# Attention scores from three 64-row products on the two halves of the matmul array, instead of two 128-row products over the whole of it

## The chip, the cores and the metric

The kernel runs on one core of a Trainium2 chip. The metric is device microseconds of one execution, the median of a few runs. TensorE (PE) does the matmuls and loads their stationary operands (PEld), VectorE (DVE), ScalarE (ACT) and GpSimd (POOL) do elementwise work, and SP issues the transfers.

## The reference

Attention with pooled queries, then two feed-forward blocks on the same 1152 tokens. Everything is float32 (some weights come as float64).

```python
def _attn_ref(q, k, v):                     # [2, 8, 1152, 64] each
    q_pool = q.reshape(B, H, S // 2, 2, D).mean(axis=3)
    scores = scale * np.matmul(q_pool, k.transpose(0, 1, 3, 2))
    scores = scores - np.max(scores, axis=-1, keepdims=True)
    attn = np.exp(scores)
    attn = attn / (np.sum(attn, axis=-1, keepdims=True) + 1e-09)
    return np.matmul(attn, v)
...
x = attn_out as [1152, 512]
x = elu(x @ w_in) @ w_out                   # 512 -> 2048 -> 512
xn = x / sqrt(mean(x * x) + 1e-6) * rms_g
out = (silu(xn @ w_gate) * (xn @ w_val)) @ w_out2   # 512 -> 1536 -> 512
```

There are 16 heads with 576 pooled queries, 1152 keys and 64 features each.

## The kernel before

**Products in parts.** A float32 operand x is split into xh, which is x rounded to the matmul's reduced type float32r, and xl = x - xh. A product x*y is then xh*yh + xh*yl + xl*yh, and where it costs nothing also xl*yl.

**Pairs and steps.** Attention works on 8 pairs of heads. A pair has 9 query tiles of 128 rows (`TILES`): four of each head, and the tile M with 64 rows of both. That is 72 steps. Step n does this, in the order in which PE gets it:

1. `emit_S`: the scores of tile n (S, L280) in one buffer `s` of 3 PSUM banks. DVE then scales them into `p` and takes the row minimum (L284). The buffer is single, so the next S waits for this L284.
2. `do_T`: 9 transposes (T, L298) of tile n - 2's exponentials, into three banks `t`; per bank ACT writes the upper part `pth` (L306) and DVE the lower part `ptl` (L68).
3. `do_AV(8)`: up to 8 matmuls (A, L324) of P^T times V for a group of tiles. A group (`GROUPS`, four per pair) takes 18 of them, in one of two banks `o`.
4. `emit_exp` (L289, ACT), then the splitting of operands of the next pair (`plan`, `do_prep`, on POOL but for the first steps), and in the last 33 steps one operation of the weight stream `ws` (lines 113 to 142) per step.

The engines' programs are in the order in which the code emits them. Between two pairs, `emit_scale` adds five transposes (L359, L360).

**Scores before.** A head's features are 64, the array has 128 rows. Queries lie twice on the partitions, keys as the upper part on partitions 0 to 63 and the lower part on 64 to 127 (`prep_k`):

```python
        hi(d, t)
        lo(d[64:128], t[64:128], d[64:128])
```

One 128-row matmul of qh with them gives qh*kh + qh*kl, and one of ql gives the other two products. A tile needs two such over 1152 keys, in three banks of 384: 6 matmuls (12 for M). Each matmul loads its stationary operand anew. Keys come in two halves of 576 columns for all 128 partitions, each half split by two operations.

**PSUM.** 8 banks: 3 for `s`, 2 for `o`, 3 for `t`; while the first two steps run, `ps1` (a second `s`) lies where `t` will be.

**After attention** the last tiles' work is mixed with the first blocks of the first feed-forward layer (`early`), and the feed-forward blocks follow (from L168 on, with 8 banks in turn).

Of the kernel before, what the change touches and what calls it, by code (L numbers as in the profile page):

```python
# [8 lines left out]
F32 = mybir.dt.float32  # L9
F32R = mybir.dt.float32r  # L10
# [27 lines left out]
def tile_kernel(ctx: ExitStack, tc: tile.TileContext, qd, kd, vd, w1d, w2d, wgd, wvd, wod, rgd, outd):  # L38
# [31 lines left out]
    NE, WB = 3, 8      # pieces split during attention; buffers for pieces' parts  # L70
# [1 line left out]
    class Stream:  # L72
        """Pieces are worked on operation by operation, so that they fill the engines' gaps."""

        def __init__(self, srcs):
            self.srcs = srcs
            self.loaded = self.done = self.at = 0
            self.alloc = False      # the next operation allocates the parts of piece self.at
            self.raw, self.parts = {}, {}
            self.pools = [(wp, NE)]     # the parts of the pieces go round their buffers  # L80
            self.ops = self.work()
# [14 lines left out]
        def work(self):  # L96
            tail = None
            for i in range(len(self.srcs)):
# [4 lines left out]
                if wide:  # L103
                    # float64 as pairs of words -> float32, rounded to nearest: the upper word's bits in float32's
                    # places, and the lower word times the exponent's power of two; under 2^-126: 0 (the upper
                    # words, read as float32, are in the order of the magnitudes).
# [42 lines left out]
        def step(self, i, k):  # L149
            """Up to k operations, with piece i the first in use."""  # L150
# [12 lines left out]
    def product(out, w, a, first, last, ks=range(4)):  # L163
        """out += sum over 4 blocks of 128 rows of w^T a, w and a in parts; a(k): the parts of block k."""
# [16 lines left out]
    def elu(ps, gh, gl, lo):  # L181
        """g = max(h, exp(min(h, 0)) - 1) in parts."""
# [10 lines left out]
    w_out = [w2d[i] for i in range(16)]      # index quad * 4 + dm  # L193

    # =================== attention ===================
# [7 lines left out]
    pp = actx.enter_context(tc.tile_pool(name="psO", bufs=1, space=PSUM))  # L203
# [3 lines left out]
    # a head's queries in parts, with 64 columns of zeros before and after; those of the tile M come first (j = 1)  # L207
    # or last (j = 0)
# [11 lines left out]
    KD, VD, QD = {}, {}, {}     # (pair, j)  # L220

    def load(kind, p, j, half=0):
# [3 lines left out]
        elif kind == "k":  # L226
# [4 lines left out]
            SP.dma_start(out=t, in_=kd[2 * p + j][:, half * QS:(half + 1) * QS])  # L231
# [5 lines left out]
    def prep_q(p, j, t, eng, cols=((0, QS),)):  # L237
        """Sums of two queries in parts."""
# [10 lines left out]
    def prep_k(p, j, half, t, eng):  # L249
        hi, lo = eng  # L250
        if half == 0:
            KD[p, j] = ap.tile([128, S], F32R, tag="kd", name="kd", bufs=3)
        d = KD[p, j][:, half * QS:(half + 1) * QS]
        hi(d, t)
        lo(d[64:128], t[64:128], d[64:128])
# [9 lines left out]
    st = {}         # pair -> statistics tile: [0] -scale*max, [1] sum, [2] sum + eps, [3] 1 / sum  # L265
    P = {}
    xf = {}

    def emit_S(p, i):
        if i == 0:  # L270
            st[p] = ap.tile([128, 4, NPT, 1], F32, tag="st", name="st", bufs=2)
        s = (tp if (p, i) == (0, 1) else sp).tile([128, 3, 512], F32, tag="s", name="s", bufs=1)
        if i == M:
            parts = [(QD[p, j][:, u, c:c + 128], KD[p, j]) for j, c in ((1, 0), (0, 576)) for u in (0, 1)]
        else:
            j, c, _, _, _ = TILES[i]
            parts = [(QD[p, j][:, u, c:c + 128], KD[p, j]) for u in (0, 1)]
        for n, (a, b) in enumerate(parts):
            for m in range(3):
                PE.matmul(s[:, m, 0:384], lhsT=a, rhs=b[:, 384 * m:384 * m + 384],  # L280
                          start=n == 0, stop=n == len(parts) - 1)
        pt = P[p, i] = ap.tile([128, 3, 384], F32, tag="p", name="p", bufs=3)
        # -scale * scores, and the least of them (scale = 1/8, and 1/2 of the mean of two queries)
        V.tensor_scalar(out=pt, in0=s[:, :, 0:384], scalar1=-0.0625, scalar2=None,  # L284
# [24 lines left out]
    class AV:  # L309
        """P^T * V for a group: the product with the upper part of V on partitions 0-63, with the lower on 64-127."""  # L310
# [5 lines left out]
        def emit(self, k):  # L316
            g = self.g
            if self.n == 0:
                self.o = pp.tile([128, 512], F32, tag="o", name="o", bufs=2)
# [418 lines left out]
```

## Time and profile before

| | us |
|---|---|
| median of 3 runs (724.67 to 725.17) | 725.07 |
| span of the profiled execution, first to last instruction | 722.7 |
| around the span (difference of the two) | 2.4 |
| first L284 to last L284, 72 steps | 9.37 to 245.93 |

The runs of the profile page are timed from outside; its own time is not listed apart, and the span with 2.4 us around it stands for it. PE is busy 689.2 us of the span, DVE 614.9, ACT 415.6 and POOL 390.7; the busy time of PE counts overlapping instructions once and holds the modelled tail of each matmul. The granted TensorE clock is a share of 2.4 GHz.

### The profile page before, as it was taken

How to read it: one execution, taken by the hardware profiler on the slowest of the kernel's cores; microseconds unless marked ns; L12 is line 12 of the kernel's file. 1: busy time of each engine (PE TensorE's matmuls, PEld its weight loads, DVE VectorE, ACT ScalarE, POOL GpSimd, SP SyncE). 2: the span in 40 equal slices, each digit the busy share in tenths (PEclk: the TensorE clock that was granted, in tenths of full speed). 3: DMA queues.
4: the chain of work that ended last, by engine and by line, in shares of the span. 5: the costliest groups of instructions: out<-in, count | busy, mean ns of one | idle time of the engine just before them, and what ended most of it. 6: DMA issues, size and time to landing. Idle time of an engine off the chain costs nothing.

```text
span 722.7 us, 11547 instructions
## 1 busy us (share of the span) xinstructions
PE 689.2 (95%) x4243; PEld 673.3 (93%) x4243; DVE 614.9 (85%) x965; ACT 415.6 (58%) x855; POOL 390.7 (54%) x326
## 2 busy tenths in 40 slices
PE   7999999999999999969999968979999999999997
PEld 6999999989899999859999968979999999999997
DVE  7988989898999869999999999955999999999700
ACT  5888988889798865663356663424444443432300
POOL 4988889788896226754335453523445544443300
PEclk9999999999999999989999998989999999999999
DMA  5333322533331001223322212200222222222300
GB/s 196 116 96 135 98 84 83 172 131 107 105 98 48 1 30 60 87 70 105 117 92 85 87 59 88 88 30 1 87 88 89 88 88 88 88 88 88 124 34 33
DMA packets 21607, 62.34 MB, mean 86 GB/s; under 512 B 2736, under 2 KB 4784, under 8 KB 21552
## 3 DMA queue, kind: packets, MB, share of 16 engines
q1 hardware_dynamic: 21552, 61.62, 25.9%
q8 instruction: 33, 0.54, 0.3%
q14 instruction: 22, 0.18, 0.1%
HBM read 59.25 MB, written 2.36 MB: 85 GB/s over the span
## 4 chain that ended last, share of the span: by engine, by line
PE 74%; DVE 19%; ACT 3%; issue 3%; DMA 1%; SPq 0%; POOL 0%; DVEq 0%; ACTq 0%; POOLq 0%
PE b L169 15%; PE b L168 15%; PE b L170 15%; PE s L280 10%; PE o L324 9%; PE t L298 8%; DVE wt L121 3%; DVE wt L118 3%; DVE p L284 2%; DVE ptl L68 2%; DVE e L188 2%; DVE wx L124 2%; DVE wx L126 1%; DVE wt L130 1%; DVE wt L113 1%
## 5 line engine op out<-in xcount | busy, mean ns | idle before, releaser
L62 POOL TENSOR_TENSOR wl<-wt,wh 128x512 fp32r<-128x512 f32 x68 | 106.1, 1561 | 111.6 <-ACT wh L142 60.2
L168 PE MATMUL b<-xh,wh 128*128 128x384 f32 x468 | 157.7, 337 | 2.1 <-DVE e L188 1.5
L170 PE MATMUL b<-xh,wl 128*128 128x384 f32 x468 | 157.3, 336 | 0.0
L169 PE MATMUL b<-xl,wh 128*128 128x384 f32 x468 | 157.1, 336 | 0.0
L284 DVE TENSOR_SCALAR_CACHE_REDUCE p<-s 128x1152 f32<-128x1152 f32 x72 | 97.2, 1352 | 17.5 <-PE s L280 17.4
L68 DVE TENSOR_TENSOR ptl<-t,pth 128x384 fp32r<-128x384 f32 x216 | 106.5, 547 | 2.7 <-ACT pth L306 2.0
L280 PE MATMUL s<-kd,qt 128*128 128x384 f32 x480 | 98.6, 343 | 5.4 <-DVE p L284 4.8
L306 ACT CAST pth<-t 128x384 fp32r<-128x384 f32 x216 | 89.2, 488 | 24.1 <-PE t L298 23.5
L121 DVE SCALAR_TENSOR_TENSOR wt<-we,wt 128x512 f32<-128x512 f32 x68 | 95.5, 1404 | 4.5 <-ACT sqm L562 0.5
L289 ACT ACTIVATE p<-p,st 128x1152 f32<-128x1152 f32 x72 | 91.4, 1269 | 5.8 <-DVE p L284 5.5
L168 PEld LDWEIGHTS b<-xh,wh 128*128 128x128 f32 x468 | 88.0, 188 | 3.5 <-DVE e L188 2.5
L280 PEld LDWEIGHTS s<-kd,qt 128*128 128x128 f32 x480 | 81.5, 188 | 9.3 <-DVE p L284 6.5
L170 PEld LDWEIGHTS b<-xh,wl 128*128 128x128 f32 x468 | 88.0, 188 | 0.3 <-POOL wl L62 0.3
L169 PEld LDWEIGHTS b<-xl,wh 128*128 128x128 f32 x468 | 88.0, 188 | 0.0
L298 PE MATMUL t<-ident,p 128*128 128x128 f32 x648 | 85.3, 275 | 0.1
L324 PE MATMUL o<-pth,vd 128*128 128x256 f32 (+1 forms) x288 | 84.4, 315 | 0.0
L298 PEld LDWEIGHTS t<-ident,p 128*128 128x128 f32 x648 | 74.0, 141 | 6.3 <-DVE ptl L68 3.9
L324 PE MATMUL o<-ptl,vd 128*128 128x256 f32 (+1 forms) x288 | 78.5, 295 | 0.0
L168 PE MATMUL b<-gh,wh 128*128 128x384 f32 x180 | 64.3, 357 | 14.1 <-ACT gh L189 10.8
L142 ACT CAST wh<-wt 128x512 fp32r<-128x512 f32 x68 | 42.1, 619 | 59.5 <-DVE wt L130 58.4
L111 ACT ACTIVATE we<-wr 128x512 f32<-128x512 f32 x68 | 45.8, 674 | 47.2 <-DMA wr<-in_w_dram 16.1
L62 POOL TENSOR_TENSOR gl<-e,gh 128x384 fp32r<-128x384 f32 x37 | 46.8, 1265 | 41.4 <-ACT gh L189 39.7
(114 smaller groups left out, 1414.5 us busy)
## 6 DMA issues: line engine op xcount, KB each, us to landing
wr<-in_w_dram SPq DMA_DIRECT2D x32, 512.0 KB, 3.2
rawk<-in_k_dram SPq DMA_DIRECT2D x32, 288.0 KB, 2.9
rawq<-in_q_dram SPq DMA_DIRECT2D x15, 576.0 KB, 3.9
wr<-in_wg_dram SPq DMA_DIRECT2D x12, 512.0 KB, 3.2
wr<-in_wv_dram SPq DMA_DIRECT2D x12, 512.0 KB, 3.2
wr<-in_wo_dram SPq DMA_DIRECT2D x12, 512.0 KB, 3.3
rawv<-in_v_dram SPq DMA_DIRECT2D x16, 288.0 KB, 2.8
out_dram<-o SPq DMA_DIRECT2D x12, 192.0 KB, 1.9
```

The lines of the kernel that those rows point to most:

```text
L62: G.tensor_tensor(out=o, in0=i, in1=f(h), op=ALU.subtract)
L68: V.tensor_tensor(out=o, in0=i, in1=f(h), op=ALU.subtract)
L121: V.scalar_tensor_tensor(out=f(t), in0=e, scalar=TINY64 * TINY64, in1=f(t), op0=ALU.is_ge, op1=ALU.mult)
L168: PE.matmul(out, lhsT=wh[:, k, :], rhs=ah, start=first and k == 0, stop=False)
L169: PE.matmul(out, lhsT=wh[:, k, :], rhs=al, start=False, stop=False)
L170: PE.matmul(out, lhsT=wl[:, k, :], rhs=ah, start=False, stop=last and k == 3)
L280: PE.matmul(s[:, m, 0:384], lhsT=a, rhs=b[:, 384 * m:384 * m + 384], start=n == 0, stop=n == len(parts) - 1)
L284: V.tensor_scalar(out=pt, in0=s[:, :, 0:384], scalar1=-0.0625, scalar2=None, op0=ALU.mult, op1=ALU.min, accum_out=st[p][:, 0, TILES[i][4], :])
L289: T.activation(out=pt, in_=pt, func=AF.Exp, scale=-1.0, bias=st[p][:, 0, TILES[i][4], :], accum_out=st[p][:, 1, TILES[i][4], :])
L298: PE.transpose(ps[:, k, :], src[:, 128 * b:128 * b + 128], ident)
L306: T.copy(oh, re(ps))
L324: PE.matmul(self.o[:, 0:self.N], lhsT=v[:, b, :], rhs=(pth, ptl)[u][:, g["buf"], b, g["c0"]:320], start=self.n == 0, stop=self.n == 17)
```

## The change

Only attention's front half changes.

- **Scores.** `kd` is now [128, 2, 576]: on partitions 0 to 63 lie the first 576 keys, on 64 to 127 the other 576, each as upper (index 0) and lower part (index 1). A score is three products over 64 rows: qh*kh, qh*kl and ql*kh; ql*kl is gone. The products of the first 576 keys use partitions 0 to 63 of queries and keys, those of the others partitions 64 to 127, and they alternate in the program; they write different banks. 288 columns go into a bank, four banks to a tile: 12 matmuls of 288 columns with 64 rows, instead of 6 of 384 columns with 128 rows.
- **Keys.** One load of two 64-partition pieces and one split (two operations) per head, instead of two loads and two splits.
- **PSUM.** `s` has four banks, `o` one; `do_AV(9)` makes each group two equal portions. The feed-forward blocks turn over 4 + 4 banks, formerly 5 + 3.
- **Start.** The 24 transposes ahead of the first scores write a tile of `tp`.

```diff
-            SP.dma_start(out=t, in_=kd[2 * p + j][:, half * QS:(half + 1) * QS])
+            for h in range(2):
+                SP.dma_start(out=t[64 * h:64 * h + 64], in_=kd[2 * p + j][64 * h:64 * h + 64, QS * h:QS * h + QS])
...
-    def prep_k(p, j, half, t, eng):
+    def prep_k(p, j, t, eng):
         hi, lo = eng
-        if half == 0:
-            KD[p, j] = ap.tile([128, S], F32R, tag="kd", name="kd", bufs=3)
-        d = KD[p, j][:, half * QS:(half + 1) * QS]
-        hi(d, t)
-        lo(d[64:128], t[64:128], d[64:128])
+        d = KD[p, j] = ap.tile([128, 2, QS], F32R, tag="kd", name="kd", bufs=3)
+        hi(d[:, 0, :], t)
+        lo(d[:, 1, :], t, d[:, 0, :])
...
-        s = (tp if (p, i) == (0, 1) else sp).tile([128, 3, 512], F32, tag="s", name="s", bufs=1)
+        s = (tp if (p, i) == (0, 1) else sp).tile([128, 4, 512], F32, tag="s", name="s", bufs=1)
...
-        for n, (a, b) in enumerate(parts):
-            for m in range(3):
-                PE.matmul(s[:, m, 0:384], lhsT=a, rhs=b[:, 384 * m:384 * m + 384],
-                          start=n == 0, stop=n == len(parts) - 1)
-        pt = P[p, i] = ap.tile([128, 3, 384], F32, tag="p", name="p", bufs=3)
+        parts = [(QD[p, j][:, u, c:c + 128], KD[p, j][:, v, :]) for j, c in parts for u, v in ((0, 0), (0, 1), (1, 0))]
+        for m in range(2):
+            for n, (a, b) in enumerate(parts):
+                for h in range(2):
+                    r = slice(64 * h, 64 * h + 64)
+                    PE.matmul(s[:, 2 * h + m, 0:288], lhsT=a[r], rhs=b[r, 288 * m:288 * m + 288],
+                              start=n == 0, stop=n == len(parts) - 1)
+        pt = P[p, i] = ap.tile([128, 4, 288], F32, tag="p", name="p", bufs=3)
...
-                self.o = pp.tile([128, 512], F32, tag="o", name="o", bufs=2)
+                self.o = pp.tile([128, 512], F32, tag="o", name="o", bufs=1)
...
-        do_AV(8, lambda p: later.append((step + 2, lambda: emit_x(p, emit_scale(p)))))
+        do_AV(9, lambda p: later.append((step + 2, lambda: emit_x(p, emit_scale(p)))))
...
-    psb = [ctx.enter_context(tc.tile_pool(name="psB", bufs=5, space=PSUM))]
+    psb = [ctx.enter_context(tc.tile_pool(name="psB", bufs=4, space=PSUM))]
```

On PE, around the tile M of the first pair, the program before reads as follows (`s` are scores, `t` transposes, `o` products with V; the shape is that of the output):

```order
L324 MATMUL o<-ptl,vd 128x320
L280 MATMUL s<-kd,qt_93 128x384 x6
L280 MATMUL s<-kd,qt_91 128x384 x6
L324 MATMUL o<-pth,vd 128x320
L324 MATMUL o<-ptl,vd 128x320
L298 MATMUL t<-ident,p 128x128 x9
L324 MATMUL o<-pth,vd 128x256
```

The same place of the changed program:

```order
L326 MATMUL o<-ptl,vd 128x320
L282 MATMUL s<-kd,qt_90 128x288 x6
L282 MATMUL s<-kd,qt_88 128x288 x6
L282 MATMUL s<-kd,qt_90 128x288 x6
L282 MATMUL s<-kd,qt_88 128x288 x6
L300 MATMUL t<-ident,p 128x128 x9
L326 MATMUL o<-pth,vd 128x256
```

The 12 score matmuls of M have become 24, and the two left-over matmuls of a group that stood ahead of the transposes have gone into the portions of 9.

At the change from one pair to the next the program before has, on PE, four matmuls ahead of the transposes and then 8 in the next step; the first rows of the changed program at that place are these:

```order
L326 MATMUL o<-ptl,vd 128x256
L300 MATMUL t<-ident,p 128x128 x9
L282 MATMUL s<-kd,qt_88 128x288 x12
L300 MATMUL t<-ident,p 128x128 x9
L282 MATMUL s<-kd,qt_88 128x288 x12
```

So one step of each pair now holds scores and transposes alone, and the other eight hold 9 products with V each.

On POOL, the keys of a head take these four rows before, and the two rows below them now:

```order
L59 TENSOR_SCALAR kd<-rawk 128x576
L62 TENSOR_TENSOR kd<-rawk,kd 64x576
L59 TENSOR_SCALAR kd<-rawk 128x576
L62 TENSOR_TENSOR kd<-rawk,kd 64x576
```

```order
L59 TENSOR_SCALAR kd<-rawk 128x576
L62 TENSOR_TENSOR kd<-rawk,kd 128x576
```

The second operation now covers 128 partitions, and there is one of each instead of two.

## Rows read from the trace of the kernel before

**Rows 1.** The profile page: busy time of the engines, then the granted clock in 40 slices of the span, and the shares of the chain that ended last.

```profile
span 722.7 us, 11547 instructions
PE 689.2 (95%) x4243; PEld 673.3 (93%) x4243; DVE 614.9 (85%) x965; ACT 415.6 (58%) x855; POOL 390.7 (54%) x326
PEclk9999999999999999989999998989999999999999
PE 74%; DVE 19%; ACT 3%; issue 3%; DMA 1%; SPq 0%; POOL 0%; DVEq 0%; ACTq 0%; POOLq 0%
```

**Rows 2.** Busy time of each engine in two pairs of heads (one without weight operations on DVE, one with), and in the stretch of all steps with weight operations. Columns: stretch, its length, busy us of PE, PEld, DVE, ACT, POOL with instruction counts, granted clock, DMA share, GB/s.

```profile
72.42:102.30 29.88, 29.88 (x220) 29.09 (x219) 25.81 (x50) 25.55 (x55) 25.30 (x25) 1.00 0.31 100
191.86:222.96 31.10, 30.26 (x218) 28.90 (x217) 29.49 (x55) 26.64 (x57) 27.77 (x26) 1.00 0.35 112
138.40:245.93 107.53, 104.79 (x749) 99.50 (x748) 102.76 (x188) 92.55 (x199) 85.82 (x76) 1.00 0.27 90
```

**Rows 3.** DVE in order of time, the score evacuations that begin a stretch: start, duration, in brackets the idle time before it and who ended it. (The first, at 19.58, is that of step 4; those at 72.42 and 102.30 are one pair apart.)

```profile
19.58 1.36 DVE L284 TENSOR_SCALAR_CACHE_REDUCE p<-s 128x1152 f32<-128x1152 f32 x1 [0.80 <-PE s L280]
...
72.42 1.36 DVE L284 TENSOR_SCALAR_CACHE_REDUCE p<-s 128x1152 f32<-128x1152 f32 x1 [1.18 <-PE s L280]
...
102.30 1.36 DVE L284 TENSOR_SCALAR_CACHE_REDUCE p<-s 128x1152 f32<-128x1152 f32 x1 [1.18 <-PE s L280]
...
138.40 1.36 DVE L284 TENSOR_SCALAR_CACHE_REDUCE p<-s 128x1152 f32<-128x1152 f32 x1 [0.21 <-PE s L280]
...
245.93 1.36 DVE L284 TENSOR_SCALAR_CACHE_REDUCE p<-s 128x1152 f32<-128x1152 f32 x1
```

**Rows 4.** DVE's idle time by group: first in the pair 72.42 to 102.30, then in the stretch 138.40 to 245.93. Columns: count, busy us, mean ns, idle us before and its releaser.

```profile
L284 DVE TENSOR_SCALAR_CACHE_REDUCE p<-s 128x1152 f32<-128x1152 f32 x10 | 13.5, 1354 | 4.7 <-PE s L280 4.7
...
L68 DVE TENSOR_TENSOR ptl<-t,pth 128x384 fp32r<-128x384 f32 x93 | 45.8, 545 | 0.8 <-ACT pth L306 0.3
L284 DVE TENSOR_SCALAR_CACHE_REDUCE p<-s 128x1152 f32<-128x1152 f32 x31 | 41.8, 1348 | 2.7 <-PE s L280 2.7
L344 DVE TENSOR_TENSOR xf<-o,olo 64x256 f32<-64x256 f32 x8 | 3.3, 411 | 1.4 <-ACT olo L343 1.4
```

**Rows 5.** PE and its weight loads in order of time, one step of the second pair: start, duration of the row's instructions together, what, count.

```profile
63.08 0.31 PE L324 MATMUL o<-pth,vd 128*128 128x320 f32 x1
63.22 0.31 PE L324 MATMUL o<-ptl,vd 128*128 128x320 f32 x1
63.22 1.04 PEld L280 LDWEIGHTS s<-kd,qt 128*128 128x128 f32 x6
63.37 1.23 PE L280 MATMUL s<-kd,qt 128*128 128x384 f32 x6
64.43 0.31 PE L324 MATMUL o<-pth,vd 128*128 128x320 f32 x1
64.58 0.31 PE L324 MATMUL o<-ptl,vd 128*128 128x320 f32 x1
64.72 1.15 PE L298 MATMUL t<-ident,p 128*128 128x128 f32 x9
```

**Rows 6.** PE in order of time, neighbouring products with V of 256 columns, and a group of scores that began after a wait.

```profile
73.73 0.28 PE L324 MATMUL o<-pth,vd 128*128 128x256 f32 x1
...
74.20 0.28 PE L324 MATMUL o<-pth,vd 128*128 128x256 f32 x1
...
154.32 1.28 PE L280 MATMUL s<-kd,qt 128*128 128x384 f32 x6 [0.32 <-DVE p L284]
...
10.78 1.34 PE L280 MATMUL s<-kd,qt 128*128 128x384 f32 x6 [0.93 <-DVE p L284]
```

**Rows 7.** Durations of single score matmuls and of transposes, minimum, median and maximum in ns.

```profile
L280 PE MATMUL s<-kd,qt x480: 331/337/670, 6.4 to 245.6; 128*128 128x384 f32 x160
L298 PE MATMUL t<-ident,p x648: 270/273/333, 12.2 to 253.7; 128*128 128x128 f32 x162
```

**Rows 8.** From scores to their evacuation and to the next scores, in order of time: the double group of a tile M on PE; and in another step the evacuation's last row on DVE.

```profile
70.11 2.27 PE L280 MATMUL s<-kd,qt 128*128 128x384 f32 x12
...
152.82 1.34 DVE L284 TENSOR_SCALAR_CACHE_REDUCE p<-s 128x1152 f32<-128x1152 f32 x1
154.10 0.08 DVE L284 DVE_READ_ACCUMULATOR p<-s 128x1 f32 x1
```

**Rows 9.** The start, in order of time: key loads on SP, the first splits on ACT and DVE, the first scores on PE, the first evacuation.

```profile
1.45 1.05 SPq L231 DMA_DIRECT2D rawk<-in_k_dram  x2
4.62 0.67 ACT L390 CAST kd<-rawk 128x576 fp32r<-128x576 f32 x1 [2.39 <-DMA rawk<-in_k_dram]
6.13 0.67 ACT L390 CAST kd<-rawk 128x576 fp32r<-128x576 f32 x1 [0.84 <-DMA rawk<-in_k_dram]
6.83 0.76 DVE L68 TENSOR_TENSOR kd<-rawk,kd 64x576 fp32r<-64x576 f32 x1 [0.76 <-ACT kd L390]
9.37 1.35 DVE L284 TENSOR_SCALAR_CACHE_REDUCE p<-s 128x1152 f32<-128x1152 f32 x1
```

**Rows 10.** POOL's splits in the pair 72.42 to 102.30: count, busy us, mean ns, idle before.

```profile
L62 POOL TENSOR_TENSOR kd<-rawk,kd 64x576 fp32r<-64x576 f32 x4 | 5.7, 1431 | 0.3
L62 POOL TENSOR_TENSOR vd<-rawv,vd 128x576 fp32r<-128x576 f32 x2 | 2.8, 1423 | 0.2
L59 POOL TENSOR_SCALAR kd<-rawk 128x576 fp32r<-128x576 f32 x4 | 2.7, 675 | 0.2
```

More of the change, by code (lines that the diff above doesn't have):

```diff
@@ L202, in tile_kernel @@
         sp = actx.enter_context(tc.tile_pool(name="psS", bufs=1, space=PSUM))
-    pp = actx.enter_context(tc.tile_pool(name="psO", bufs=1, space=PSUM))
     tctx = ExitStack()
@@ L220, in tile_kernel, with load @@
     KD, VD, QD = {}, {}, {}
-    def load(kind, p, j, half=0):
+    def load(kind, p, j):
         if kind == "q":
@@ L271, in emit_S @@
             st[p] = ap.tile([128, 4, NPT, 1], F32, tag="st", name="st", bufs=2)
-        s = (tp if (p, i) == (0, 1) else sp).tile([128, 3, 512], F32, tag="s", name="s", bufs=1)
+        s = (tp if (p, i) == (0, 1) else sp).tile([128, 4, 512], F32, tag="s", name="s", bufs=1)
         if i == M:
-            parts = [(QD[p, j][:, u, c:c + 128], KD[p, j]) for j, c in ((1, 0), (0, 576)) for u in (0, 1)]
+            parts = [(1, 0), (0, 576)]
         else:
-            j, c, _, _, _ = TILES[i]
-            parts = [(QD[p, j][:, u, c:c + 128], KD[p, j]) for u in (0, 1)]
-        for n, (a, b) in enumerate(parts):
-            for m in range(3):
-                PE.matmul(s[:, m, 0:384], lhsT=a, rhs=b[:, 384 * m:384 * m + 384],
-                          start=n == 0, stop=n == len(parts) - 1)
-        pt = P[p, i] = ap.tile([128, 3, 384], F32, tag="p", name="p", bufs=3)
-        V.tensor_scalar(out=pt, in0=s[:, :, 0:384], scalar1=-0.0625, scalar2=None,
+            parts = [TILES[i][:2]]
+        parts = [(QD[p, j][:, u, c:c + 128], KD[p, j][:, v, :]) for j, c in parts for u, v in ((0, 0), (0, 1), (1, 0))]
[6 more added lines that the diff above has]
+        pt = P[p, i] = ap.tile([128, 4, 288], F32, tag="p", name="p", bufs=3)
+        V.tensor_scalar(out=pt, in0=s[:, :, 0:288], scalar1=-0.0625, scalar2=None,
                         op0=ALU.mult, op1=ALU.min, accum_out=st[p][:, 0, TILES[i][4], :])
@@ L399, in fetch @@
             raws[u] = load(*u)
-    plan = {1: lambda p: ("v", p, 0), 2: lambda p: ("q", p + 1, 1), 3: lambda p: ("k", p + 1, 1, 0),
-            4: lambda p: ("k", p + 1, 1, 1), 5: lambda p: ("v", p + 1, 1), 6: lambda p: ("q", p + 1, 0),
-            7: lambda p: ("k", p + 1, 0, 0), 8: lambda p: ("k", p + 1, 0, 1)}
+    plan = {1: lambda p: ("v", p, 0), 2: lambda p: ("q", p + 1, 1), 4: lambda p: ("k", p + 1, 1),
+            5: lambda p: ("v", p + 1, 1), 6: lambda p: ("q", p + 1, 0), 7: lambda p: ("k", p + 1, 0)}
     steps = [(p, i) for p in range(8) for i in ([0, 1, 3, 4, 2, 5, 6, 7, 8] if p == 0 else range(NPT))]
@@ L410, in tile_kernel @@
         if p == 0:
-            u = {0: [("k", 0, 0, 1)], 2: [("v", 0, 1)], 3: [("v", 0, 0)]}.get(k, [])
+            u = {2: [("v", 0, 1)], 3: [("v", 0, 0)]}.get(k, [])
             jobs[n] += u
@@ L421, in tile_kernel @@
     SP.dma_start(out=t[:, :, 64:320], in_=q01[:, :, 64:320])
-    fetch(("k", 0, 1, 0))
-    fetch(("k", 0, 1, 1))
+    fetch(("k", 0, 1))
     for a, b in ((320, 576), (0, 64)):
         SP.dma_start(out=t[:, :, a:b], in_=q01[:, :, a:b])
-    first = [("q", 0, 0), ("k", 0, 0, 0)]
+    first = [("q", 0, 0), ("k", 0, 0)]
     for u in first + order[:1]:
         fetch(u)
-    warm = pp.tile([128, 512], F32, tag="o", name="warm", bufs=2)
+    warm = tp.tile([128, 4, 512], F32, tag="s", name="warm", bufs=1)
     for n in range(24):
-        PE.transpose(warm[:, 0:128], ident, ident)
+        PE.transpose(warm[:, 0, 0:128], ident, ident)
     prep_q(0, 1, t, DVE, ((64, 320),))
-    do_prep(("k", 0, 1, 0), ACT)
-    do_prep(("k", 0, 1, 1), ACT)
+    do_prep(("k", 0, 1), ACT)
     prep_q(0, 1, t, DVE, ((320, 576), (0, 64)))
@@ L479, in tile_kernel @@
             tp = actx.enter_context(tc.tile_pool(name="psT", bufs=1, space=PSUM))
+            pp = actx.enter_context(tc.tile_pool(name="psO", bufs=1, space=PSUM))
             tbank = lambda: tp.tile([128, 512], F32, tag="t", name="t", bufs=3)
@@ L501, in tile_kernel @@
         ws.step(0, step >= ns - 33)
-    fb = sp.tile([128, 3, 512], F32, tag="s", name="fb", bufs=1)
+    fb = sp.tile([128, 4, 512], F32, tag="s", name="fb", bufs=1)
     def early(n, ks=range(4)):
@@ L539, in bank @@
         n, nbank = nbank % 8, nbank + 1
-        if n == 5 and len(psb) == 1:
+        if n == 4 and len(psb) == 1:
             with tc.using_default_side("right"):
-                psb.append(ctx.enter_context(tc.tile_pool(name="psC", bufs=3, space=PSUM)))
-        return psb[n >= 5].tile([128, 512], F32, tag="b", name="b", bufs=3 if n >= 5 else 5)[:, 0:CH]
+                psb.append(ctx.enter_context(tc.tile_pool(name="psC", bufs=4, space=PSUM)))
+        return psb[n >= 4].tile([128, 512], F32, tag="b", name="b", bufs=4)[:, 0:CH]
     gh, gl = (gp.tile([128, 8, NT], F32R, name=f"g{n}", tag=f"g{n}") for n in "hl")
```

## The prediction, made before the changed kernel was run

> **What bounds the kernel now.** I read the page first, then stretches, then single steps. The page says that PE is busy 95% of the span and carries 74% of the last chain, at the full clock nearly everywhere [rows 1]. The change touches attention alone, so the share that counts is attention's. Its 72 steps have two regimes. Up to about 138 us a pair of heads takes 102.30 - 72.42 = 29.88 us [rows 3], and PE is busy in all of it while DVE has 25.81 us of work and stands idle for scores, 4.7 us in that pair [rows 2, 4]. From 138.40 on the weight stream adds work to DVE: it is busy 102.76 of 107.53 us, a pair takes 31.10 us, and PE is busy only 30.26 of those [rows 2]. So the first regime, 138.40 - 19.58 = 118.8 us or 4.0 pairs [rows 3], is bound by PE and follows it. The second, 245.93 - 138.40 = 107.5 us or 3.4 pairs, is bound by DVE, which waits 0.8 + 2.7 + 1.4 = 4.9 us in all of it [rows 4]: that is the most that a faster PE can bring there, and about 1.2 us a pair is what a slower PE may cost before it shows.
>
> How PE spends a step shows in one of them [rows 5]. Products with V follow each other after 0.146 us at 320 columns (63.08, 63.22), and after 0.47 / 4 = 0.117 us at 256 [rows 6]; that is 0.46 ns a column, and 0.132 us at 288. Six scores last 1.23 us together, the last of them 0.337 [rows 7], so they follow after (1.23 - 0.337) / 5 = 0.179 us; by the column slope from 320 it would be 0.175, which I take. Nine transposes of 128 columns last 1.15 with 0.273 for the last, 0.110 us apart [rows 5, 7]. That is far above 0.117 less 128 x 0.46 ns, 0.058 us: transposes wait for their weight loads, and a load of 128 columns takes 0.11 us of the path. A group that begins after a wait shows the same 0.11 bare: 1.34 us against 1.23 [rows 5, 6].
>
> **The change part by part, for one pair.** A pair has nine score groups and one of them double, so 10 units.
>
> *Scores.* Before: 10 x 6 x 0.175 = 10.5 us. After there are 12 matmuls a unit on half the rows. If the two halves stream at the same time, a unit takes 6 x 0.132 = 0.79 us and a pair 7.9: **2.6 us less**. If only the streams of a half overlap and the weight loads queue on one path, a unit takes 12 x 0.11 = 1.32 us, 2.7 more in a pair. If nothing overlaps, 12 x 0.132 = 1.58 us, 5.3 more. The trace has no matmul on fewer than 128 rows, so nothing in it chooses. I take the first: the halves use different rows of the array, different partitions of both operands and different banks, and today a load is hidden behind a stream wherever the stream is longer than 0.11 (the load at 63.22 starts with the matmul before it [rows 5]); 0.132 still is.
>
> The Trainium skill, "TensorEngine Tiling (Array Packing)", Key Properties, says that different tiles can execute weight loads and matmuls in parallel, which would be this first case; no run here shows it.
>
> *Changes between 128 and 64 rows.* Each step goes from whole-array work to half-array work and back: 18 changes a pair. Today neither the way into a group (63.22 to 63.37) nor out of it costs anything [rows 5], so the lower bound is 0. The upper bound is that the array must finish and the next weights load bare: the matmul's tail, 0.337 - 0.175 = 0.16, and the load's 0.11, 0.27 us each, 4.9 a pair. I take one bare load per step, 9 x 0.11 = **1.0 us more**, nearer to today's nothing: a half can take its next weights while the other streams, but 128-row weights need both halves.
>
> The Trainium skill, "TensorEngine Tiling (Array Packing)", Key Properties, also says that changing the tiling mode, not just the tile, drains TensorE. The trace has no such change, so it neither agrees nor disagrees; the upper bound is what it would mean here, and it stands below as a rival.
>
> *Nines instead of eights.* Eight steps have 9 products with V and one has none. In that one PE has 0.79 + 9 x 0.11 + 0.11 = 1.89 us, while the single score buffer forces a chain from scores to scores: the group (5 x 0.132 + 0.337 = 1.0), 0.04 to the evacuation (70.11 + 2.27 = 72.38, and 72.42), its 1.36, and 0.13 until the next scores (154.18 to 154.32, [rows 6, 8]): 2.53 us. PE stands for **0.65 us more**. With one bank `o` a group waits for the copies of the last; a whole score group and nine transposes (1.8 us) lie between, and an addition takes 0.41 [rows 4] and a copy, by estimate, as long, so that costs nothing; without that cover it would be 0.8 four times a pair.
>
> *Evacuation and exponentials* handle the same 1152 columns and cost the same; DVE and ACT gain and lose nothing there.
>
> *Keys.* POOL does two of each operation a pair instead of four: (5.7 + 2.7) / 2 = 4.2 us less [rows 10], on 128 partitions at the same 1.42 us (the `vd` row). POOL is busy 25.30 of 29.88 us, PE does not wait for it, so this is worth nothing in the first regime. In the second it can shorten DVE's weight operations where the two disturb each other; I put it into the term there. Half the key bytes: the loads are hidden already. SP's queue has one issue less a head pair and nothing queues behind it.
>
> *Start.* DVE's splits of the second key half, 0.76 us, and ACT's wait for its load (6.13 against 4.62, 1.5 us later) stand ahead of the first evacuation at 9.37, which DVE reaches after the query splits behind them [rows 9]. With one split this comes about 1.5 us earlier, less 0.1 for the second piece's issue: **1.4 us less**, bounds 0 and 2.2 (the queue of POOL's splits after it shortens too).
>
> **The sum.** First regime: 2.6 - 1.0 - 0.65 = 0.95 a pair, 3.8 in four. Second: of at most 4.9 I take 1.0, since DVE stays the bound. Start 1.4. Together 6.2 us. The profiled execution is 722.7 us of span and 2.4 around, which is the median, 725.1; so **719 us**. Nothing after attention changes but the turn of the banks, 4 + 4, which costs nothing while the first blocks are read within the 8 us that four banks last (4 x 12 matmuls x 0.175).
>
> **The rivals.**
>
> *Full change-over.* Each of the 18 changes costs 0.27: 4.9 instead of 1.0 a pair. The empty step then waits only some 0.2. That is 2.6 - 4.9 - 0.2 = 2.5 more a pair, 10 in the first regime; in the second 2.3 - 1.2 = 1.1 a pair, 4; less the start 1.4: about **738 us**. It decides the sign where a change costs more than about 0.13. For it: a wide array that is reconfigured must be empty somewhere, and PE has no slack in the first regime. Against it: changes between transposes, V products and scores cost nothing today, but those all use the whole array. By the skill's rule on the drain this would be the outcome, with 0.27 as the most that it costs.
>
> *Weight loads on one path.* A unit is 1.32 instead of 1.05: 2.7 more a pair, and the empty step waits about 0.8. First regime 3.5 to 4.5 (with bare loads) x 4 = 14 to 18, second 1.5 to 2.5 x 3.4 = 5 to 8, start -1.4: **742 to 749 us**. For it: transposes run at the pace of their loads, one per 0.11 us, and no row has two loads closer. Against it: those all go to the same rows.
>
> *No overlap at all*, the change doing nothing that it says: 5.3 + 0.65 a pair, 24 and 14, so about **762 us**. Nothing in the rows excludes it.
>
> *A draw.* Changes at about 0.13 us each, or DVE at once the bound: between 723.6 and 726.5, that is within 0.2%, about what this measurement can tell from nothing.
>
> **Chances.** Halves together with cheap changes 0.45 (own range 713 to 723: the low end is free changes, 2.6 - 0.65 = 1.95 a pair, 8, with 1.4 at the start and 2.5 in the second regime); draw 0.10; full change-over 0.21; loads on one path 0.17; no overlap 0.07. Faster 0.45, same 0.10, slower 0.45. The range 713 to 747 leaves out the case without overlap and the worst of the one-path case, some 0.15.
>
> **What will show it.** Right: score matmuls of the two halves starting within a few ns of each other, pairs of them about 0.13 us apart, a group of twelve about 1.0 us long in the timeline; the transposes that follow starting about 0.1 later than a usual spacing; a pair of heads near 29 us up to 138 us; one step a pair with PE idle on DVE's evacuation; first evacuation near 8 us. Wrong: matmuls 0.11 apart (one path) or 0.13 apart (no overlap) in single file; gaps of 0.2 and more on both sides of each score group (change-over); DVE busy in the whole of the first regime. It would also be wrong if the evacuation over four banks took longer than 1.36, which would lengthen the chain in every step.

## The result, and the profile after

The changed kernel takes 729.45 us (median; 728.12 to 732.17), the one before 725.08 beside it: a ratio of 1.0052, interval 1.0032 to 1.0073. It is slower by half a per cent, where 719 was forecast. The ratios here and below leave out single executions of over 1000 us, of which some sets of runs hold one. The profiled execution after takes 730.07 us with a span of 728.3, 5.6 us more than before.

The page after (span, busy times, granted clock in 40 slices, shares of the last chain), to be held against [rows 1]:

```profile
span 728.3 us, 12507 instructions
PE 689.5 (95%) x4723; PEld 658.2 (90%) x4723; DVE 613.0 (84%) x964; ACT 414.9 (57%) x853; POOL 359.0 (49%) x297
PEclk9999999999999999999999998989999999999999
PE 70%; DVE 21%; issue 3%; ACT 3%; DMA 1%; SPq 1%; POOL 0%; DVEq 0%; ACTq 0%
```

POOL lost 32 us of work and PE's busy sum stayed, yet PE's share of the last chain fell from 74 to 70% and DVE's rose from 19 to 21%, which fits that PE now waits for DVE more often.

The evacuations that begin the stretches, as in [rows 3] (step 4, one pair's ends, steps 40 and 71), and the windows of [rows 2]:

```profile
20.37 1.36 DVE L286 TENSOR_SCALAR_CACHE_REDUCE p<-s 128x1152 f32<-128x1152 f32 x1 [0.56 <-PE s L282]
...
74.66 1.36 DVE L286 TENSOR_SCALAR_CACHE_REDUCE p<-s 128x1152 f32<-128x1152 f32 x1 [1.15 <-PE s L282]
...
105.38 1.36 DVE L286 TENSOR_SCALAR_CACHE_REDUCE p<-s 128x1152 f32<-128x1152 f32 x1 [1.16 <-PE s L282]
...
142.45 1.36 DVE L286 TENSOR_SCALAR_CACHE_REDUCE p<-s 128x1152 f32<-128x1152 f32 x1
...
251.37 1.36 DVE L286 TENSOR_SCALAR_CACHE_REDUCE p<-s 128x1152 f32<-128x1152 f32 x1 [0.53 <-PE s L282]
```

```profile
74.66:105.38 30.72, 30.02 (x279) 26.98 (x280) 25.91 (x49) 25.67 (x56) 21.06 (x22) 1.00 0.26 78
142.45:251.37 108.92, 104.20 (x951) 93.59 (x952) 100.62 (x187) 92.91 (x199) 70.77 (x64) 0.98 0.23 70
```

Against before, step 4 comes 20.37 - 19.58 = 0.8 us later, the first regime (20.37 to 142.45) takes 122.1 instead of 118.8, 3.3 more, the second 108.9 instead of 107.5, 1.4 more, and the rest 0.2 more: 5.6 in all. A pair takes 30.72 instead of 29.88. PE is no longer busy throughout it, but idle for 0.70.

**The halves do run at the same time.** First the score matmuls that start between 93.12 and 93.30 us (durations in ns, then first and last start), then one step on PE and on its weight loads, in order of time:

```profile
L282 PEld LDWEIGHTS s<-kd,qt x4: 183/185/187, 93.1 to 93.2; 64*128 64x128 f32 x4
L282 PE MATMUL s<-kd,qt x2: 396/397/398, 93.1 to 93.1; 64*128 64x288 f32 x2
```

```profile
92.74 0.31 PE L326 MATMUL o<-ptl,vd 128*128 128x320 f32 x1
92.89 0.31 PE L326 MATMUL o<-pth,vd 128*128 128x320 f32 x1
93.12 0.83 PEld L282 LDWEIGHTS s<-kd,qt 64*128 64x128 f32 x12 [0.19 <-issue]
93.13 1.06 PE L282 MATMUL s<-kd,qt 64*128 64x288 f32 x12
94.12 0.42 PEld L300 LDWEIGHTS t<-ident,p 128*128 128x128 f32 x4 [0.17 <-issue]
94.12 1.20 PE L300 MATMUL t<-ident,p 128*128 128x128 f32 x9
95.08 0.40 PE L326 MATMUL o<-ptl,vd 128*128 128x320 f32 x1
```

Two matmuls and two pairs of loads share their starts; by the trace's single records the halves of this step start 1 to 6 ns apart, the second pair comes 0.24 us after the first, and the others follow every 0.13 us. Twelve take 1.06 us. But the way in and the way out now cost something. Before, scores followed a product with V after its usual 0.15 us, and their first load started with it [rows 5]. Here they come 0.24 us after the product at 92.89, their load after 0.19 us in which the load path did nothing, and the transposes' load after 0.17 us of the same.

**The empty step.** The step without products with V and the scores that wait behind it, on PE and DVE, in order of time:

```profile
86.78 1.06 PE L282 MATMUL s<-kd,qt 64*128 64x288 f32 x12
86.87 1.49 DVE L68 TENSOR_TENSOR ptl<-t,pth 128x384 fp32r<-128x384 f32 x3
...
88.27 1.35 DVE L286 TENSOR_SCALAR_CACHE_REDUCE p<-s 128x1152 f32<-128x1152 f32 x1
...
89.68 1.06 PE L282 MATMUL s<-kd,qt 64*128 64x288 f32 x12 [0.70 <-DVE p L286]
```

That is the wait that the prediction named: 0.70 us until the single score buffer is evacuated. From scores to scores the step takes 2.90 us (86.78 to 89.68). The scores end at 87.84, but their evacuation starts only at 88.27, behind DVE's work on the transposes.

### The profile page after: what moved, and what is told of

It reads as the page before. It is cut to its first block, busy times and chain, and to the rows that moved or that the text cites. A ratio compares the mean times of both kernels' runs of the same rounds, so it can differ in the third digit from the quotient of the medians.

```text
span 728.3 us, 12507 instructions
## 1 busy us (share of the span) xinstructions
PE 689.5 (95%) x4723; PEld 658.2 (90%) x4723; DVE 613.0 (84%) x964; ACT 414.9 (57%) x853; POOL 359.0 (49%) x297
## 3 DMA queue, kind: packets, MB, share of 16 engines
HBM read 54.53 MB, written 2.36 MB: 78 GB/s over the span
## 4 chain that ended last, share of the span: by engine, by line
PE 70%; DVE 21%; issue 3%; ACT 3%; DMA 1%; SPq 1%; POOL 0%; DVEq 0%; ACTq 0%
PE b L168 13%; PE b L169 13%; PE b L170 13%; PE o L326 10%; PE s L282 9%; PE t L300 8%; DVE wt L121 4%; DVE wt L118 3%; DVE e L188 2%; DVE wx L126 2%; DVE wx L124 2%; DVE p L286 2%; DVE ptl L68 2%; DVE wt L130 1%; DVE wt L113 1%
## 5 line engine op out<-in xcount | busy, mean ns | idle before, releaser
L282 PE MATMUL s<-kd,qt 64*128 64x288 f32 x960 | 83.8, 309 | 8.9 <-DVE p L286 8.8
L300 PE MATMUL t<-ident,p 128*128 128x128 f32 x648 | 87.8, 282 | 2.1 <-ACT p L291 2.1
L282 PEld LDWEIGHTS s<-kd,qt 64*128 64x128 f32 x960 | 66.7, 186 | 21.9 <-DVE p L286 11.4
L300 PEld LDWEIGHTS t<-ident,p 128*128 128x128 f32 x648 | 71.4, 143 | 12.7 <-issue 7.5
L326 PE MATMUL o<-pth,vd 128*128 128x256 f32 (+1 forms) x288 | 80.6, 304 | 0.1
L326 PE MATMUL o<-ptl,vd 128*128 128x256 f32 (+1 forms) x288 | 80.4, 304 | 0.0
```

Source lines behind the costliest of these rows:

```text
L282: PE.matmul(s[:, 2 * h + m, 0:288], lhsT=a[r], rhs=b[r, 288 * m:288 * m + 288], start=n == 0, stop=n == len(parts) - 1)
L300: PE.transpose(ps[:, k, :], src[:, 128 * b:128 * b + 128], ident)
L326: PE.matmul(self.o[:, 0:self.N], lhsT=v[:, b, :], rhs=(pth, ptl)[u][:, g["buf"], b, g["c0"]:320], start=self.n == 0, stop=self.n == 17)
```

## The experiments

**What the change of array shape costs.** The first run puts the scores' 64-row halves back into whole-array matmuls of the same length and leaves all else as changed.

```diff
-                for h in range(2):
-                    r = slice(64 * h, 64 * h + 64)
-                    PE.matmul(s[:, 2 * h + m, 0:288], lhsT=a[r], rhs=b[r, 288 * m:288 * m + 288],
-                              start=n == 0, stop=n == len(parts) - 1)
+                h = n % 3 == 1
+                PE.matmul(s[:, 2 * h + m, 0:288], lhsT=a, rhs=b[:, 288 * m:288 * m + 288],
+                          start=n < 2, stop=n >= len(parts) - 2)
```

> The changed kernel, but a score group is 6 matmuls of 288 columns over all 128 rows (12 for the tile M) instead of 12 on two halves; everything else, the four banks, the split of the keys, the nines, stays. The sums mix the two halves of the keys, so this kernel leaves the right scores out and its time alone counts. The streams take the same time as the overlapping pairs (6 x 0.133 us), and no step changes between 128 and 64 rows. Theory A (the changes of array shape eat the gain, about 0.34 us a step by the spacings in the trace of the changed kernel, 0.09 drained and 0.11 bare load on the way in, 0.09 and 0.06 on the way out): a pair of heads falls from 30.7 us to about 27.8 in the first regime, and the whole to 729.4 - 10 to 13 = 716 to 719 us. Theory B (the step with scores alone and the chain through the single score buffer hold the pair, changes are cheap): the pair stays at 30 or above, 726 us or more.

Measured: 716.81 us, 0.9887 of before (0.9872 to 0.9902). The window of one pair:

```profile
69.98:98.13 28.15, 27.42 (x220) 26.80 (x219) 25.62 (x50) 25.29 (x56) 21.12 (x21) 1.00 0.28 85
```

28.15 against 30.72: 2.57 us a pair is what 18 changes of shape cost, 0.143 each. Its PE at the same kind of place shows where:

```profile
86.89 0.31 PE L325 MATMUL o<-pth,vd 128*128 128x320 f32 x1
87.03 0.95 PE L281 MATMUL s<-kd,qt 128*128 128x288 f32 x6
87.83 1.14 PE L299 MATMUL t<-ident,p 128*128 128x128 f32 x9
88.73 0.39 PE L325 MATMUL o<-ptl,vd 128*128 128x320 f32 x1
```

Product to scores takes 0.14 us (after: 0.24), scores to transposes 0.80 (0.99), transposes to products 0.90 (0.96): 1.84 against 2.19, 0.35 us a step for two changes. Of the 0.19 us between scores and transposes, by single records, 0.10 lie between the first pair of halves and the second, and 0.09 in front of the first transpose. The step that waits for the evacuation pays nothing: from scores to scores it takes 2.90 us after and 3.08 in this run (80.75 to 83.83). Eight times 0.35 less 0.18 is 2.6, the pair's difference. This run also halves the number of matmuls and loads; the next one leaves it as it was and still pays.

The second run keeps the halves and doubles the changes: one of the nine transposes moves between the two banks' worth of each score group.

```diff
-    def emit_S(p, i):
+    def emit_S(p, i, mid=None):
...
+            if m == 0 and mid:
+                emit_T0(*mid)
```

> The changed kernel with one of the nine transposes of each step moved between the first 6 and the last 6 score matmuls of that step: the same work, two more changes of array shape in 70 of the 72 steps. Theory A: 0.3 to 0.35 us more a step where PE is the bound, so 3 us more a pair, 12 in the first four pairs and less than that in the others, 740 to 752 us in all. Theory B: changes are cheap, under 3 us more.

Measured: 754.71 us, 1.0404 (1.039 to 1.0419). One pair's window, and a step on PE:

```profile
81.81:115.56 33.75, 33.16 (x279) 27.52 (x280) 26.00 (x50) 25.73 (x55) 21.08 (x21) 1.00 0.23 71
```

```profile
90.79 0.67 PE L282 MATMUL s<-kd,qt 64*128 64x288 f32 x6
91.39 0.33 PE L301 MATMUL t<-ident,p 128*128 128x128 f32 x1
91.65 0.66 PE L282 MATMUL s<-kd,qt 64*128 64x288 f32 x6
92.24 0.66 PE L373 MATMUL t<-ident,rs 128*128 128x128 f32 x4
```

33.75 - 30.72 = 3.03 us for 18 more changes, 0.168 each. In the rows, two half groups with a transpose between them take 92.24 - 90.79 = 1.45 us; a whole group (0.99) and a transpose (0.11) take 1.10: 0.35 for two changes again. Two runs that differ in opposite directions agree on 0.14 to 0.17 us. The time is above the range that was expected, 740 to 752.

**What the single bank and the nines cost.** The kernel before, with its 128-row scores, gets one bank `o` and nine products a step:

```diff
-                self.o = pp.tile([128, 512], F32, tag="o", name="o", bufs=2)
+                self.o = pp.tile([128, 512], F32, tag="o", name="o", bufs=1)
...
-        do_AV(8, lambda p: later.append((step + 2, lambda: emit_x(p, emit_scale(p)))))
+        do_AV(9, lambda p: later.append((step + 2, lambda: emit_x(p, emit_scale(p)))))
```

> The kernel before with one bank for P*V and portions of 9, the scores as they were. It prices that part of the change alone: one step a pair without products with V. Predicted with the change was 0.65 us a pair, 2.6 in the first four pairs; with scores of 6 x 0.175 the empty step has 1.05 + 0.98 us of PE against a chain of 0.107 + 5 x 0.175 + 0.337 + 0.04 + 1.36 + 0.13 = 2.85, so 0.8 a pair, 3 us in four, and a little in the others: 727 to 729 us. Rival: later steps make up for it, since PE has 0.5 us of slack a pair already: the time of before within 0.7 us.

Measured: 729.70 us, 1.0058 (1.0046 to 1.0071); the nines alone cost as much as the whole change, and a little more than was expected. Two further runs fill the empty step, one in the changed kernel, one in the kernel before with one bank: the first group goes in sixes, so that its products reach into the step that had none.

```diff
-        do_AV(9, lambda p: later.append((step + 2, lambda: emit_x(p, emit_scale(p)))))
+        do_AV(6 if avq and avq[0].g is GROUPS[0] else 9, lambda p: later.append((step + 2, lambda: emit_x(p, emit_scale(p)))))
```

> The changed kernel, with the one group of a pair that has a free step behind it (the first of the four) done in three portions of 6 instead of two of 9, so that no step is left with scores and transposes alone. Still one bank for P*V. Theory D (the empty step is what the nines cost): 0.6 us less a pair in the first regime and about as much in the second, 729.4 - 3.5 to 4.5 = 725 to 726 us, that is the time of before: the shorter scores and the changes of array shape cancel, 2.4 against 2.6 us a pair. Rival (one bank for P*V costs by itself, in the wait for its copies): 728 us or more.

> The kernel before with one bank for P*V and the portions of 9, but the first group in portions of 6: beside the run with nines it removes the empty step alone. Theory D: back to the time of before, 725.2 within 0.8 us. Rival: the single bank costs, 728 to 730 us.

Measured: 726.47 us in the changed kernel, 1.0009 (0.9998 to 1.0021), and 726.33 in the one before, 1.0007 (0.9995 to 1.0018). Both are a little above the times expected, and the same as the kernel before beside them (725.44). One pair in the nines, in the sixes of before, and in the sixes of the changed kernel:

```profile
73.73:104.24 30.51, 29.78 (x220) 29.20 (x219) 26.00 (x50) 25.67 (x55) 25.33 (x25) 1.00 0.30 98
```

```profile
72.90:102.63 29.73, 29.73 (x220) 29.27 (x219) 25.99 (x49) 25.77 (x55) 25.24 (x25) 1.00 0.32 100
```

```profile
73.34:103.30 29.96, 29.96 (x279) 27.04 (x280) 26.00 (x49) 25.76 (x56) 21.07 (x22) 1.00 0.26 80
```

The number behind the comma is PE's busy time. With nines PE rests 0.73 us a pair, with sixes not at all. The empty step costs 30.51 - 29.73 = 0.78 us with the old scores and 30.72 - 29.96 = 0.76 with the new. The single bank by itself costs nothing in a pair of the first regime (29.73 against 29.88 before). In the second regime this is not shown: the kernel before takes 107.5 us from step 40 to step 71, and 109.0 with one bank and the sixes.

**What the start costs.** The keys come as two transfers of 64 partitions after the change. This run lays them out so that one transfer of 128 partitions brings the same bytes.

```diff
-            for h in range(2):
-                SP.dma_start(out=t[64 * h:64 * h + 64], in_=kd[2 * p + j][64 * h:64 * h + 64, QS * h:QS * h + QS])
+            SP.dma_start(out=t, in_=kd[2 * p + j])
```

> The changed kernel with the keys laid out on the host as [128, 576] a head, so that one transfer over 128 partitions brings them instead of two over 64. Theory C (the start is late because the two 64-partition pieces land late: the first key cast on ACT at 5.70 us instead of 4.62, the second head's at 11.38 instead of 10.22, and ACT's first exponential stands behind that one, at 11.96; PE then idles 2.1 us and its clock falls): casts at about 4.6 and 10.2, first exponential near 10.8, no lower clock at 13 to 16 us, step 3's evacuation at about 15 instead of 17.05, and 2 to 3 us less in all, about 727. Rival: the pieces are not what is late, and nothing moves by more than 0.5 us.

Measured: 728.37 us, 1.0037 (1.0024 to 1.0051), some 1.1 us less than the changed kernel, where 2 to 3 were expected; the intervals of the two ratios overlap. The two profiles differ by 2.0 us, but step 4's evacuation comes only 0.44 us earlier (19.93 against 20.37), and 0.95 us lie in the second regime. The start of the changed kernel itself (ACT's casts and first exponentials, DVE's first evacuation, PE's first transposes, two windows):

```profile
5.70 0.67 ACT L392 CAST kd<-rawk 128x576 fp32r<-128x576 f32 x1 [3.47 <-DMA rawk<-in_k_dram]
...
8.83 1.35 DVE L286 TENSOR_SCALAR_CACHE_REDUCE p<-s 128x1152 f32<-128x1152 f32 x1
...
11.38 0.67 ACT L392 CAST kd<-rawk 128x576 fp32r<-128x576 f32 x1 [5.01 <-DMA rawk<-in_k_dram]
11.96 1.25 ACT L291 ACTIVATE p<-p,st 128x1152 f32<-128x1152 f32 x1
...
13.36 1.91 PE L300 MATMUL t<-ident,p 128*128 128x128 f32 x9 [2.06 <-ACT p L291]
```

```profile
12.00:15.00 3.00, 1.64 (x9) 1.50 (x9) 0.80 (x3) 3.00 (x7) 2.83 (x4) 0.78 0.00 0
15.00:18.00 3.00, 3.00 (x23) 2.49 (x21) 2.38 (x4) 2.98 (x7) 1.02 (x2) 0.65 0.86 282
```

The first cast waits until 5.70 (4.62 before [rows 9]) and the second, of the other head's keys, until 11.38. The first exponentials stand behind that cast in ACT's queue. The evacuation they need had ended at 10.18, so 1.8 us of a head start are lost. PE waits 2.06 us, and in the two windows its granted clock is 0.78 and 0.65, each a mean over time at its two levels: nine transposes take 1.91 us instead of 1.2. With one transfer the casts came at 4.59 and 10.10, but PE still rested, 1.47 us before the first transposes, and the clock between 12 and 18 us was 0.50.

The next two runs were a first try to give PE work in that wait, and the plain combination of sixes and one transfer.

```diff
+    def keep(n):
+        w = pp.tile([128, 512], F32, tag="o", name="keep", bufs=1)
+        for _ in range(n):
+            PE.transpose(w[:, 0:128], ident, ident)
```

> The changed kernel with the portions of 6, the keys in one load, and 32 extra transposes of the identity in the waits of steps 2 and 3, into the idle P*V bank, so that TensorE does not rest long enough for its clock to fall at the start. If the clock at 9 to 18 us is what the start still lacks, it stays at 1.00 there, step 3's evacuation comes at about 14.5 us (16.03 with one load alone, 15.75 before), and the whole takes 722 to 724 us, 1 to 3 less than the kernel before. If the extra transposes only take PE's time, 725 us or more.

> The changed kernel with the first group's products with V in sixes and each head's keys in one transfer of 128 partitions, no extra transposes. Theory A: the two parts add (the empty step -3.0 us, the key pieces -1.1), about 725.4 us, with PE idle about 1.5 us before the first transposes and a granted clock near 0.5 between 12 and 18 us. Theory B: the pieces' 1.1 us is not there once the sixes are in: about 726.5.

Measured: 727.12 us with `keep`, 1.0022 (1.0011 to 1.0032), and 724.25 without, 0.9984 (0.9972 to 0.9995). The first try decided nothing: the bank `o` is one of those that the second step's scores hold at the start, so the 14 transposes waited for that evacuation, started at 11.25, and pushed the third step's scores to 13.73. The combination was better than theory A had it. In its profiled execution the second key cast came at 9.26, PE waited only 0.40 us for its first transposes, and the clock stayed at 1.00.

So the extra transposes went into columns of the score banks that nothing reads, first in three batches, then in two; beside the latter the plain combination ran again.

```diff
+        for _ in range({(0, 1): 14, (0, 3): 6}.get((p, i), 0)):
+            PE.transpose(s[:, 3, 384:512], ident, ident)
```

> As the run beside it, and 14, 12 and 6 extra transposes of the identity behind the scores of steps 1, 2 and 3, written into columns of the score banks that nothing reads, so that PE has work while it waits for the first evacuations and exponentials. Theory A: the fall of the clock at the start is what the first steps lose against before; with PE fed the granted clock stays at 1.00 from 9 to 18 us, the fourth evacuation comes near 15.0 instead of 16.0 us, and the time is about 1 us less, 724.5. Theory B: the first steps wait for the exponentials on ACT whatever PE does; the clock stays up, the fourth evacuation comes within 0.3 us of the run beside it, and the time is the same.

> Sixes, one key transfer, and extra transposes of the identity behind the scores of the second step (14) and of the third (6) only; the batch of 12 that stood behind the double scores and held the evacuation back by 1.74 us is gone. Theory A: feeding PE keeps the clock up in the first steps in every execution; the fourth evacuation comes near 15.1 us where the key cast is at 10.1, the eleventh near 37.2, and the time is 1 us under the sixes with one load (724.25), 723.3. Theory B: the extra transposes hold back the third evacuation by as much as the clock gives (0.49 us stood there in the run before), and the time is 724 to 725.

> The sixes with one key load once more, with its own profile beside the run above: if the landing of the second key load varies from execution to execution (9.26 and 10.10 us for its cast so far), this profile may show the late one, with the clock down to about 0.5 between 12 and 18 us, the fourth evacuation near 16.0 instead of 14.21 us, and about 725 us; a cast near 9.3 again would say that the transfer is what the extra transposes disturb.

Measured: 726.22 us with three batches (1.0007, 0.9998 to 1.0016), 724.30 with two (0.9984, 0.9975 to 0.9993), 725.33 with none (0.9989, 0.9977 to 1.0001). In the first of these the batch of 12 stood behind the double scores of M, not behind the third step's as its expectation says, and held DVE for 1.74 us before the evacuation at 19.83. The other two are the clean pair. With two batches (two windows with the clock in the third column from the right, and the fourth evacuation):

```profile
12.00:15.00 3.00, 2.79 (x25) 2.24 (x26) 2.11 (x5) 3.00 (x8) 2.69 (x2) 1.00 0.25 36
15.00:18.00 3.00, 2.28 (x26) 1.88 (x27) 2.82 (x6) 3.00 (x7) 1.43 (x1) 1.00 0.73 260
```

```profile
15.19 1.35 DVE L287 TENSOR_SCALAR_CACHE_REDUCE p<-s 128x1152 f32<-128x1152 f32 x1
```

And without them:

```profile
12.00:15.00 3.00, 2.68 (x13) 2.36 (x15) 1.15 (x4) 2.81 (x8) 2.78 (x2) 0.50 0.22 28
15.00:18.00 3.00, 3.00 (x21) 2.67 (x17) 2.28 (x4) 2.56 (x6) 1.09 (x1) 0.50 0.70 273
```

```profile
16.28 1.36 DVE L285 TENSOR_SCALAR_CACHE_REDUCE p<-s 128x1152 f32<-128x1152 f32 x1 [0.67 <-PE s L281]
```

The second key cast came at 10.23 in the one and 10.34 in the other, so the transfer is not the difference. PE waited 1.68 us without the batches, the clock fell to 0.50, and the fourth evacuation came 1.09 us later. So the batches keep the clock up. What that is worth in the whole time is not shown: the intervals of the two ratios overlap, the profiled spans differ by 0.7 us (722.7 and 723.4), and the plain combination ran at 724.25 us in one set of runs and at 725.33 in another. Three executions of the second set had a mean granted clock of 0.986 and took 723.2 to 723.8 us, six had 0.979 to 0.983 and took 724.8 to 726.0. With the batches ten of eleven had 0.985 or 0.986, and took 723.4 to 725.0: the batches hold the clock, but where it holds without them the plain kernel is no slower. They also hold the third evacuation back (11.53 against 10.71 us), as theory B said. In the plain combination's two profiles the second key cast came at 9.26 with the clock up and at 10.34 with it down, which fits a loss that depends on when the keys land; two profiles do not show more. The version with two batches takes 0.16% off the kernel before. That is clear of 1 by its interval, and about as much as the two sets of the plain combination differ (1.1 us); leaving aside the first experiment, whose scores are others, no version was faster by more.

## Why the prediction was wrong

**Halves at the same time: right.** Starts, spacing (0.13 from the second pair on) and group length (1.06 against "about 1.0") came as said. The scores' gain is 30.51 - 28.15 = 2.36 us a pair, whole-array scores of 288 columns against the old ones in the same frame of nines; 2.6 was forecast. The two rivals that needed single file are out.

**The changes of shape: the step that failed.** The prediction took "one bare load per step, 9 x 0.11 = 1.0 us more", between bounds of 0 and 4.9. The changes cost 2.57, so with 2.36 gained the scores became a draw and not a gain of 1.6. The bare load was meant for the way out, and 0.15 us was measured there (0.09 in front of the first transpose, 0.06 between the first two). The way in was left at today's nothing and costs 0.20: 0.10 before the first pair of halves, and 0.10 between it and the second. The argument that a half can take its next weights while the other streams did not hold there: the load path did nothing for 0.19 us, and the second pair came after 0.24 us instead of 0.13. The rival "full change-over" had the mechanism, with 0.27 a change, and named 0.13 as the point from which it decides; 0.14 to 0.17 was measured. So the time lies between draw and that rival's 738.

The Trainium skill, "TensorEngine Tiling (Array Packing)", Key Properties, says that changing the tiling mode drains TensorE. The rows agree in that every change costs, 0.143 and 0.168 us each in the two runs, less than the bound of 0.27. The Trainium skill's other rule there, that tiles load weights and multiply in parallel, agrees with the common starts at 93.13.

**Nines: right in the first regime.** 0.65 was forecast, 30.51 - 29.88 = 0.63 measured; the empty step alone is 0.78, against the sixes. In the changed kernel the wait of 0.70 us is near the forecast by luck: the chain from scores to scores takes 2.90 us and not 2.53, since the evacuation stands behind other work of DVE, and PE's own part takes 2.20 (86.78 to 88.98, with the modelled tail of its last transpose) and not 1.89. That the single bank is hidden was right too, in this regime. What was not weighed is that this price could be avoided, since a group of 18 need not go as 9 + 9.

**First regime.** 2.36 - 2.57 - 0.63 = -0.84 us a pair. This sum is the difference of 29.88 and 30.72 by its making, since the three terms are differences of the same windows, and so is no check of its own. Four pairs are -3.4, and the rows show -3.3 instead of +3.8.

**Second regime: the gain did not come.** The prediction held DVE for the bound, with some 1.2 us a pair of room for a slower PE, and put down 1.0 us of gain. But [rows 2] have PE busier there than DVE, 104.79 against 102.76 of 107.53 us, and in the pair shown PE rests 31.10 - 30.26 = 0.84 us, not 1.2. The stretch took 1.4 us more, and 0.95 of this is one fall of the clock. In the changed kernel, on DVE, PE and in a window:

```profile
149.74 1.73 DVE L118 SCALAR_TENSOR_TENSOR wt<-wr,wt 128x512 uint32<-128x512 uint32 x1
...
152.79 1.13 PE L282 MATMUL s<-kd,qt 64*128 64x288 f32 x12 [2.35 <-DVE p L286]
...
153.85 2.18 PE L300 MATMUL t<-ident,p 128*128 128x128 f32 x9
```

```profile
154.00:156.00 2.00, 2.00 (x10) 2.00 (x11) 2.00 (x3) 1.14 (x4) 1.86 (x2) 0.50 0.55 147
```

A long weight operation on DVE falls into the empty step, PE rests 2.35 us, and the clock is granted at 0.50 behind it: nine transposes take 2.18 us. In the run with one key transfer the same step rests as long, and the clock stays up; its PE there, and its stretch from step 40 to step 71:

```profile
152.34 1.06 PE L281 MATMUL s<-kd,qt 64*128 64x288 f32 x12 [2.35 <-DVE p L285]
153.33 1.20 PE L299 MATMUL t<-ident,p 128*128 128x128 f32 x9
```

```profile
142.00:249.97 107.97, 102.77 (x951) 92.13 (x952) 100.47 (x187) 92.71 (x199) 71.09 (x64) 1.00 0.22 71
```

So with the clock up the stretch takes 107.97 us, 0.4 more than before, where 0.84 a pair over 3.4 pairs (31 steps) would be 2.9: most of a slower PE is hidden there, as the prediction had it. The sixes take 108.06, so in the changed kernel the empty step costs nothing in this regime. The room has an end: with twice the changes the stretch took 120.26 us, 12.3 more than 107.97, and 3.03 a pair would be 10.4 (its granted clock was 0.97 on average). What was wrong is the gain. Even with whole-array scores there was little, though a pair takes 1.7 us less in the first regime:

```profile
132.13:237.93 105.80, 97.56 (x747) 91.72 (x745) 103.15 (x188) 91.97 (x199) 71.80 (x64) 1.00 0.23 72
```

That is 1.7 us under the old time, with DVE busy 103.15 of 105.80 us; that this floor is DVE's work is likely by its share, but no run shows it by itself. What the remaining 0.4 us against before are was not tried.

**Start: wrong in sign.** The first evacuation came at 8.83 us and not near 8 (8.14 with one transfer), but this was not what the next steps waited for. The prediction followed the first evacuation to DVE and stopped there; late next were the exponentials behind a cast in ACT's queue, and then PE at the lower clock. Half the bytes in 64-partition pieces were counted as "the loads are hidden already", which holds for the steps but not for the first two heads.

Summed: -6.2 us were forecast and +5.6 came in the profiled execution. Of the 11.8 between them, the first regime holds 7.1, the second 2.4, the start up to step 4 2.2, and the rest of the span 0.2. Of the second regime's part, 0.95 is the fall of the clock in this one execution.

## What to carry to other kernels

A TensorE group that uses another array shape than its neighbours pays on entering and on leaving, here some 0.3 us together, so a gain of 0.3 us in the group is gone; count the changes before the columns. Portions of work should be cut so that every step keeps some, because where PE is the bound a step without it shows the whole chain through a single buffer. At a start, follow each saved microsecond to the next engine's queue, and look whether PE rests longer before its next work.

## What was not expected of the hardware

- A matmul on 64 rows does not stream faster or slower than one on 128: 288 columns follow each other every 0.13 us in halves, and in 0.80 / 6 = 0.133 with the whole array.
- Weight loads of both halves, 0.184 us each in the records, share the time as their matmuls do; six pairs lie in 0.83 us.
- In six profiles PE rested 1.47 to 2.21 us before its first transposes, and the granted clock fell to its lower level (1.2 GHz) behind the rest; after rests of 0.40, 0.71 and 1.30 us at the same place it stayed at 1.00. The length of the rest does not settle it: after 2.35 us in the same step of two profiles the clock fell in one and stayed up in the other, 0.95 us apart over the stretch.
- At the start a head's keys were cast later when they came in two pieces of 64 partitions than in one of 128 partitions with as many bytes: the first head's at 5.70 to 6.05 us in four profiles against 4.59 to 4.70 in six, the second head's at 11.37 to 11.67 against 9.26 to 10.34.
